# Five products instead of three ahead of batch 1's first kv, batch 3's third x block one slot earlier, and the late q groups transposed by DMA instead of TensorE

## The chip, the cores and the metric

One core of a Trainium2 chip. The metric is the device time of one execution in microseconds (us), lower is better, as the median of several runs. A profile is one execution taken by the hardware profiler; its times count from the start of its span. PE is TensorE, PEld its weight loads, DVE is VectorE, ACT is ScalarE, POOL is GpSimd, SP is the engine that issues most DMAs.

## The reference, cut to what matters

```python
# q, k, v: (8 batches, 8 heads, 576, 64); x: 4608 tokens x 512
q_s = softmax over the head dimension of q
k_s = softmax over the sequence of k
kv  = einsum('bhsd,bhse->bhde', k_s, v)
x   = einsum('bhsd,bhde->bhse', q_s, kv)      # to (tokens, 512)
h = x @ w_in                                  # 512 -> 2048
g = h + sin(alpha * h)**2 / alpha
out = g @ w_out                               # 2048 -> 512
```

## The kernel before: the parts that matter

The 4608 tokens go through the two-layer part in nine blocks of 512 ("layer blocks", `t`). The attention of a later batch is woven into the layer work of an earlier block. A "slot" is one of the sixteen 128-row pieces of h: four matmuls on PE, a sine on ACT, a square on ACT, POOL or DVE as a string of letters says, and a combine on DVE, which also frees the PSUM buffer of that h. The "kv" of a batch is its small product of k and v, an "x block" is one of four pieces of a batch's attention output x, and an "output product" is one matmul of g with w_out.

```python
def h_slot(t, ni, sq, lag, wide=None):
    hp = mm_h(t, ni, wide, 2 if t < 2 and ni < 2 else 0)      # 4 matmuls, 512 columns each
    lag.append((t, ni, hp, sine(t, ni, hp, sq)))              # ACT sine, then the square

def flush(lag, keep):
    while len(lag) > keep:
        combine(*lag.pop(0))                                  # DVE
...
        exp_to(A["qe", 1][:, 7:J], q78)          # batch 1: the last two of nine q groups come late
        take(os, 3)                              # three output products of layer block 0
        kv_mm(1, 0, ps_e, split=True)            # needs ACT's cast of the first half of v
        kv_norm(1, 0, 1)
        take(os, 3)
        kv_mm(1, 1, ps_e, split=True)
...
        norm_late(1, 7)                          # DVE: softmax of the late q groups
        load("q", q, 3)
        load("k", k, 3)
...
    take(os, 10)                                 # ten output products of layer block 1
    tp = ps_a.tile([128, 2, 2, 128], BF16, name="tp", tag="a")
    for ii in range(2):
        for j in range(2):
            nc.tensor.transpose(tp[:, ii, j], A["qe", 1][:, 7 + j, ii * 128:(ii + 1) * 128], identb)
    DVE_CP(A["qT", 1][:, :, 7:J], tp)
    take(os, 7)
...
    def attn_back(b, n, engs=(DVE_CP, DVE_CP), xs=(4, 6, 8, 10)):
        if n == 0:
            kv_mm(b, 0, ps_a)
            kv_mm(b, 1, ps_a)
            kv_norm(b)
        elif n in xs:                            # four x blocks, all in the one buffer of ps_a
            m = xs.index(n)
            attn_out(b, m // 2, m % 2, ps_a, engs[m % 2])
...
    SQ2 = "PAPPAPAPPAPAPPAP"
    for ni in range(nN):                         # layer block 2
        h_slot(2, ni, SQ2[ni], lag, lent)
        flush(lag, 2)
        attn_back(3, ni - 5, (DVE_CP, ACT_CP), (5, 7, 9, 10))
    flush(lag, 0)
```

After layer block 2, ACT loads the table for the exponential, takes the exponentials of batch 4's q and k, loads the table for the sine and starts on layer block 3. PE meanwhile starts the slots of layer block 3 in the four PSUM buffers there are; its fifth slot needs the first one combined.

The softmax here doesn't subtract the row's maximum and nothing guards it: scores larger than these inputs give would overflow.

Of the kernel before, what the change touches and what calls it, by code (L numbers as in the profile page):

```python
# [16 lines left out]
BF16 = mybir.dt.bfloat16  # L17
# [6 lines left out]
def kernel(  # L24
# [14 lines left out]
    nc = tc.nc  # L39
# [5 lines left out]
    J = 9  # L45
# [20 lines left out]
    identb = singles.tile([128, 128], BF16, name="identb")  # L66
# [10 lines left out]
    def src_view(t, b):  # L77
        return t[b].rearrange("(i e) (p j) d -> (e p) i (j d)", e=2, j=J)
# [7 lines left out]
    def load(name, t, b, halves=False, eng=nc.sync, gate=None):  # L86

        st = stage.tile([128, 4, J, D], F32, name=f"st_{name}", tag="st")
        for ii in range(2) if gate else ():
            gate(st[:, ii, 0, 0:1], zero)  # L90
        view = src_view(t, b)
        flat = st.rearrange("p i j d -> p i (j d)")
        if halves:
            for ii in range(2):
                eng.dma_start(out=flat[:, ii::2], in_=view[:, ii::2])
        else:
            eng.dma_start(out=flat, in_=view)
        staged[name, b] = st

    def load_batch(b):  # L100
        load("q", q, b)
        load("k", k, b)
        load("v", v, b)
# [6 lines left out]
    def load_wout(c):  # L110
        nc.gpsimd.dma_start(out=wout[:, 4 * c:4 * c + 4, :], in_=wout_v[:, 4 * c:4 * c + 4, :])


    A = {}

    def exp_to(dst, src, iis=range(2)):
        for ii in iis:
            nc.scalar.activation(dst[:, :, ii * 128:(ii + 1) * 128].rearrange("p j (x d) -> p x j d", x=2),  # L118
                                 src[:, ii::2], AX.Exp)
# [5 lines left out]
    def exp_half(name, b, ii, j1=J):  # L125
        if ii == 0:
            A[name + "e", b] = att2.tile([128, J, 4 * D], BF16, name=name + "e")
        exp_to(A[name + "e", b][:, 0:j1], staged[name, b][:, :, 0:j1], (ii,))

    def exp_k(b):  # L130
        A["ke", b] = att2.tile([128, J, 4 * D], BF16, name="ke")
        exp_to(A["ke", b], staged["k", b])
# [22 lines left out]
    def norm_late(b, j0):  # L155

        qe = A["qe", b][:, j0:J].rearrange("p j (i d) -> p j i d", i=4)
        qs = small.tile([128, J, 4], F32, name="qs")[:, j0:J]
        nc.vector.tensor_reduce(qs, qe, axis=AXL.X, op=ALU.add)
        nc.vector.reciprocal(qs, qs)  # L160
        nc.vector.tensor_tensor(qe, qe, qs.unsqueeze(3).to_broadcast([128, J - j0, 4, D]), op=ALU.mult)
# [119 lines left out]
    ACT_CP, DVE_CP, GP_CP = nc.scalar.copy, nc.vector.tensor_copy, nc.gpsimd.tensor_copy  # L281
# [4 lines left out]
    def load0(eng, n, t, ii, j0=0, j1=J):  # L286
        eng.dma_start(out=staged[n, 0][:, ii::2, j0:j1].rearrange("p i j d -> p i (j d)"),
                      in_=src_view(t, 0)[:, ii::2, j0 * D:j1 * D])
# [80 lines left out]
    def h_slot(t, ni, sq, lag, wide=None):  # L369
        hp = mm_h(t, ni, wide, 2 if t < 2 and ni < 2 else 0)  # L370
        lag.append((t, ni, hp, sine(t, ni, hp, sq)))

    def flush(lag, keep):
        while len(lag) > keep:
            combine(*lag.pop(0))

    def o_quad(t, accs, engs):

        R = range(4)
        by_m, by_n = [(n, m) for m in R for n in R], [(n, m) for n in R for m in R]  # L380
        orders = [by_m, by_n, by_n, by_m]
        for c in R:
            for n, m in orders[c]:
                mm_o(t, m, 4 * c + n, accs[m])
                if c == 3 and n == 3:
                    evac_o(t, m, accs[m], engs[m])
                yield

    def take(it, n=1000):
        for _ in range(n):  # L390
            if next(it, 0) == 0:
                return
# [4 lines left out]
    with ES:  # L397
        def lent():
            return ps_e.tile([128, 2, MF], F32, name="hh", tag="a")[:, 0]

        def load_q8():
            for ii in range(2):
                load0(nc.sync, "q", q, ii, 8, 9)

        def load_q1():
            staged["q", 1] = st = stage.tile([128, 4, J, D], F32, name="st_q", tag="st")
            for ii in range(2):
                DVE_CP(st[:, ii, 0, 0:1], zero)
            for ii in range(2):
                nc.sync.dma_start(out=st[:, ii::2, 0:7].rearrange("p i j d -> p i (j d)"),  # L410
                                  in_=src_view(q, 1)[:, ii::2, 0:7 * D])

        late = {4: load_q8, 6: load_q1, 8: lambda: load_wout(2),
                10: lambda: load_wout(3), 13: lambda: load("k", k, 1, halves=True, gate=DVE_CP)}
        for ni in range(nN):
            h_slot(0, ni, "DPPAPPAPPPAPPAPP"[ni], lag, lent)
            flush(lag, 1)
            if ni in late:
                late[ni]()
        flush(lag, 0)  # L420

        accs = [ps_h.tile([128, dm], F32, name="hp", tag="h") for _ in range(4)]
        os = o_quad(0, accs, [DVE_CP, ACT_CP, DVE_CP, DVE_CP])
        take(os, 46)
        exp_to(A["qe", 0][:, 8:9], staged["q", 0][:, :, 8:9])
        for ii in range(2):
            exp_half("q", 1, ii, 7)
        load("v", v, 1, halves=True)
        nc.sync.dma_start(out=q78.rearrange("p i j d -> p i (j d)"), in_=src_view(q, 1)[:, :, 7 * D:J * D])
        load_batch(2)  # L430
        norm_late(0, 8)
        norm_q(1, [GP, V], 7)
        exp_k(1)
        q_tile(1)
        for ii in range(2):
            tp = ps_e.tile([128, 16, 128], BF16, name="tp", tag="a")
            q_transpose_ii(1, ii, 0, 7, tp)
            if ii == 1:
                for i2 in range(2):
                    nc.tensor.transpose(tp[:, 8 + i2], A["qe", 0][:, 8, i2 * 128:(i2 + 1) * 128], identb)  # L440
            DVE_CP(A["qT", 1][:, ii, 0:7], tp[:, 0:7])
        DVE_CP(A["qT", 0][:, :, 8], tp[:, 8:10])
        take(os, 6)
        xp = ps_e.tile([128, 4, P], F32, name="xp", tag="a")
        for c in range(4):
            attn_chunk(0, c, 8, 9, xp[:, c])
        DVE_CP(xT[:, :, 8 * P:9 * P], xp)
        cast_v(1, [ACT_CP, DVE_CP])
        exp_to(A["qe", 1][:, 7:J], q78)
        take(os, 3)  # L450
        kv_mm(1, 0, ps_e, split=True)
        kv_norm(1, 0, 1)
        take(os, 3)
        kv_mm(1, 1, ps_e, split=True)
        kv_norm(1, 1, 2)
        take(os, 1)

        c0 = J * P
        for ii in range(2):
            xp = ps_e.tile([128, 2, 512], F32, name="xp", tag="a")[:, :, 0:7 * P]  # L460
            for e in range(2):
                attn_chunk(1, 2 * ii + e, 0, 7, xp[:, e])
            (ACT_CP, DVE_CP)[ii](xT[:, 2 * ii:2 * ii + 2, c0:c0 + 7 * P], xp)
            if ii == 0:
                nc.scalar.activation(zero, zero, AX.Sin)
            take(os, 2)
        take(os)
        norm_late(1, 7)
        load("q", q, 3)
        load("k", k, 3)  # L470

        for ki in range(2):
            for ni in range(2):
                mm_h(1, ni, lent, ki, ki + 1)
        for ni in range(nN):
            h_slot(1, ni, SQ[ni], lag, lent)
            flush(lag, 1)
        cast_v(2, [GP_CP, GP_CP])
        flush(lag, 0)

    ps_o = ctx.enter_context(tc.tile_pool(name="ps_o", bufs=2, space=PSUM, reuse_waits="tile"))
    ps_a = ctx.enter_context(tc.tile_pool(name="ps_a", bufs=1, space=PSUM, reuse_waits="tile"))
# [13 lines left out]
    exp_k(2)  # L496
    os = o_stream(1)
    take(os, 10)
    tp = ps_a.tile([128, 2, 2, 128], BF16, name="tp", tag="a")
    for ii in range(2):  # L500
        for j in range(2):
            nc.tensor.transpose(tp[:, ii, j], A["qe", 1][:, 7 + j, ii * 128:(ii + 1) * 128], identb)
    DVE_CP(A["qT", 1][:, :, 7:J], tp)
    take(os, 7)
    xp = ps_a.tile([128, 4, 2 * P], F32, name="xp", tag="a")
    for c in range(4):
# [31 lines left out]
# [5 lines that stand above are left out]
        elif n in xs:  # L543
            m = xs.index(n)
            attn_out(b, m // 2, m % 2, ps_a, engs[m % 2])
# [5 lines left out]
    for ni in range(nN):  # L551
        h_slot(2, ni, SQ2[ni], lag, lent)
        flush(lag, 2)
        attn_back(3, ni - 5, (DVE_CP, ACT_CP), (5, 7, 9, 10))
    flush(lag, 0)

    for t in range(3, nT):
        b = t + 1 if t + 1 < B else None
        os = o_stream(t - 1)
# [59 lines left out]
```

## Time and profile before

| | before |
|---|---|
| median time, first three runs | 287.75 us (287.33 to 288.11) |
| span of the profile | 285.8 us |
| PE busy | 95% |
| granted TensorE clock | 0.999 |
| PE waits after the start-up that the change aims at | 0.44 us (first kv of batch 1), 0.28 us (last x block of batch 3) |

PE is the bound in sum, so an idle tenth of a microsecond on PE is one in the total, unless a later wait of PE swallows it. Where that happens is not seen in sums: one has to lay the instructions of PE, ACT and DVE side by side. A wait in brackets behind an instruction is idle time of its engine just before it, and what ended it.

### The profile page before, as it was taken

What the parts mean: (1) busy time and instruction counts of PE and PEld (TensorE: products, weight loads), DVE (VectorE), ACT (ScalarE), POOL (GpSimd) and SP (SyncE); (2) the same over time, 40 slices, a digit from 0 to 9 for tenths busy, and PEclk for the clock granted to TensorE, in tenths of its full rate; (3) what the DMA queues carried; (4) which work ended last, traced back from release to release, by engine and by line L of the source; (5) the groups of instructions that cost most, each with busy time, mean ns of one, the idle gap of its engine ahead of it and who ended that gap; (6) DMA issues with size and microseconds to landing.
All of it is one profiled execution on the core that took longest, in us unless ns stands there. A gap on an engine that the chain in (4) does not pass through costs nothing.

```text
span 285.8 us, 4247 instructions
## 1 busy us (share of the span) xinstructions
PE 272.6 (95%) x1541; PEld 130.8 (46%) x1569; DVE 192.6 (67%) x291; ACT 226.0 (79%) x321; POOL 80.6 (28%) x75
## 2 busy tenths in 40 slices
PE   2899999999999999999999999999999999999994
PEld 1444454445454454444544454445444444444443
DVE  4857967999999658766785677667674555555321
ACT  4898748999489999899889988998877777777400
POOL 2869512773477480005300530041000000000000
PEclk9999999999999999999999999999999999999999
DMA  7999999843999984139711990016011111111242
GB/s 261 308 204 243 260 397 407 312 169 78 275 222 412 372 169 105 37 69 406 218 38 39 359 292 20 22 36 155 1 39 37 37 37 39 37 38 41 46 100 73
DMA packets 38581, 45.77 MB, mean 160 GB/s; under 512 B 16528, under 2 KB 22432, under 8 KB 38560
## 3 DMA queue, kind: packets, MB, share of 16 engines
q1 hardware_dynamic: 33376, 40.57, 46.3%
q0 software_dynamic: 4992, 4.79, 9.7%
q8 instruction: 12, 0.20, 0.3%
q10 hardware_dynamic: 192, 0.14, 0.2%
q14 instruction: 9, 0.07, 0.1%
HBM read 36.71 MB, written 9.44 MB: 161 GB/s over the span
## 4 chain that ended last, share of the span: by engine, by line
PE 74%; DVE 9%; DMA 7%; ACT 4%; issue 3%; POOL 2%; SPq 0%; ACTq 0%
PE op L268 33%; PE hp L248 33%; DMA st_v<-in_v_dram 5%; ACT s L254 3%; DVE g L264 2%; POOL s L258 2%; PE kvp L171 2%; DVE qs L150 2%; PE xp L220 2%; DMA st_q<-in_q_dram 1%; PE op L589 1%; PE hh L248 1%; DVE vb L137 1%; DVE qn L152 1%; DVE kbd L184 1%
## 5 line engine op out<-in xcount | busy, mean ns | idle before, releaser
L264 DVE SCALAR_TENSOR_TENSOR g<-s,inva_sb,hp 128x512 bf16<-128x512 f32 x130 | 96.0, 745 | 58.4 <-ACT s L256 54.2
L248 PE MATMUL hp<-xT,win 128*128 128x512 bf16 x512 | 129.0, 379 | 0.5
L268 PE MATMUL op<-wout,g 128*128 128x512 bf16 x479 | 121.9, 379 | 1.2 <-issue 0.6
L254 ACT ACTIVATE s<-hp,alpha_sb 128x512 f32<-128x512 f32 x130 | 87.8, 682 | 25.1 <-PE hp L248 22.6
L248 PEld LDWEIGHTS <-win 128*128 128x128 bf16 x576 | 56.3, 98 | 67.5 <-issue 0.8
L268 PEld LDWEIGHTS <-g 128*128 128x128 bf16 x560 | 54.1, 98 | 61.1 <-issue 0.4
L256 ACT ACTIVATE s<-s 128x512 f32<-128x512 f32 x111 | 69.9, 630 | 3.5
L152 POOL TENSOR_TENSOR qn<-qe,qs 128x1152 bf16<-128x1152 bf16 (+1 forms) x12 | 24.9, 2091 | 78.6 <-DVE qs L146 69.2
L258 POOL TENSOR_TENSOR s<-s 128x512 f32<-128x512 f32 x30 | 33.0, 1111 | 22.3 <-ACT s L254 22.0
L274 DVE COPY o<-op 128x512 f32<-128x512 f32 (+2 forms) x33 | 22.0, 668 | 9.7 <-PE op L268 5.8
L118 ACT ACTIVATE ke<-st_k 128x1152 bf16<-128x1152 f32 x16 | 17.9, 1151 | 5.0 <-DMA st_k<-in_k_dram 5.0
L118 ACT ACTIVATE qe<-st_q 128x1152 bf16<-128x1152 f32 (+3 forms) x18 | 17.7, 1025 | 2.1 <-DMA st_q<-in_q_dram 1.9
L145 DVE TENSOR_REDUCE qs<-qe 128x36 f32<-128x2304 bf16 x5 | 12.8, 2553 | 8.7 <-ACT qe L118 8.6
L268 PE MATMUL hp<-wout,g 128*128 128x512 bf16 x62 | 14.8, 379 | 0.2 <-issue 0.2
L223 DVE CAST xT<-xp 128x512 bf16<-128x512 f32 (+1 forms) x18 | 13.4, 742 | 0.0
L137 POOL CAST vb<-st_v 128x1152 bf16<-128x1152 f32 x10 | 11.3, 1163 | 6.5 <-DMA st_v<-in_v_dram 6.5
L171 PEld LDWEIGHTS <-ke 64*128 64x128 bf16 x288 | 8.4, 93 | 4.9 <-issue 1.9
L171 PE MATMUL kvp<-vb,ke 64*128 64x130 bf16 x288 | 9.9, 216 | 0.7 <-ACT vb L137 0.4
L118 ACT ACT_TABLE_LOAD x7 | 9.0, 1283 | 1.3 <-PEq L603 1.2
L248 PE MATMUL hh<-xT,win 128*128 128x512 bf16 x39 | 9.6, 379 | 0.1
L220 PE MATMUL xp<-qT,kbd 128*128 128x256 bf16 (+1 forms) x40 | 8.2, 286 | 0.4 <-DVE xT L223 0.3
L150 DVE TENSOR_REDUCE qs<-qe 128x16 f32<-128x1024 bf16 (+2 forms) x6 | 7.2, 1197 | 1.8 <-ACT qe L118 1.8
(79 smaller groups left out, 123.1 us busy)
## 6 DMA issues: line engine op xcount, KB each, us to landing
out_dram<-o SPq DMA_DIRECT2D x70, 128.0 KB, 2.3
st_q<-in_q_dram SPq DMA_DIRECT2D x6, 1152.0 KB, 6.7
st_k<-in_k_dram SPq DMA_DIRECT2D x6, 1152.0 KB, 8.9
st_v<-in_v_dram SPq DMA_DIRECT2D x6, 1152.0 KB, 10.2
st_k<-in_k_dram SPq DMA_DIRECT2D x4, 576.0 KB, 7.1
wout<-in_moe_w_out_dram POOLq DMA_DIRECT2D x4, 512.0 KB, 11.7
st_v<-in_v_dram SPq DMA_DIRECT2D x3, 576.0 KB, 9.4
win<-in_moe_w_in_dram POOLq DMA_DIRECT2D x6, 256.0 KB, 7.7
```

The costliest lines, as they stand in the source:

```text
L118: nc.scalar.activation(dst[:, :, ii * 128:(ii + 1) * 128].rearrange("p j (x d) -> p x j d", x=2), src[:, ii::2], AX.Exp)
L137: engs[ii](vv[:, 2 * ii:2 * ii + 2, :, 0:D], staged["v", b][:, ii::2])
L152: engs[ii % len(engs)].tensor_tensor(qn[:, ii, 0:j1].rearrange("p j (x d) -> p j x d", x=2), qe[:, ii], part.unsqueeze(3).to_broadcast([12 ...
L171: nc.tensor.matmul(kvp[:, e, ii * 130:(ii + 1) * 130], ke[r, j, ii * 128:(ii + 1) * 128], vt[r, j, ii * 130:(ii + 1) * 130], start=(j == 0 ...
L220: nc.tensor.matmul(xp[:, e, 0:n], kt[:, e, ii], qT[:, ii, j0:j1, e * 64:(e + 1) * 64], start=True, stop=True)
L248: nc.tensor.matmul(hp, win[:, ki, ni * 128:(ni + 1) * 128], xT[:, ki, t * MF:(t + 1) * MF], start=(ki == 0), stop=(ki == 3))
L254: nc.scalar.activation(s, hp, AX.Sin, scale=alpha_sb[:, ni:ni + 1])
L256: nc.scalar.activation(s, s, AX.Square)
L258: nc.gpsimd.tensor_tensor(s, s, s, op=ALU.mult)
L264: nc.vector.scalar_tensor_tensor(G[t][:, ni], in0=s, scalar=inva_sb[:, ni:ni + 1], in1=hp, op0=ALU.mult, op1=ALU.add)
L268: nc.tensor.matmul(acc, G[t][:, ni, j * 128:(j + 1) * 128], wout[:, ni, :], start=(ni == 0), stop=(ni == nN - 1))
L274: eng(o[:, cols], acc)
```

## The change

Its intent is to close two PE holes and to take four transposes off PE. Part 1 puts five instead of three products ahead of the kv that waits for v. Part 2 has the late q groups transposed by DMA. Part 3 moves the third x block of batch 3 one slot forward, so that the fourth need not wait for its copy.

```diff
         exp_to(A["qe", 1][:, 7:J], q78)
-        take(os, 3)
+        take(os, 5)
         kv_mm(1, 0, ps_e, split=True)
         kv_norm(1, 0, 1)
-        take(os, 3)
+        take(os, 2)
         kv_mm(1, 1, ps_e, split=True)
@@
         norm_late(1, 7)
+        for j in range(7, J):
+            nc.sync.dma_start(out=A["qT", 1][:, :, j], in_=A["qe", 1][:, j], transpose=True)
         load("q", q, 3)
@@
     take(os, 10)
-    tp = ps_a.tile([128, 2, 2, 128], BF16, name="tp", tag="a")
-    for ii in range(2):
-        for j in range(2):
-            nc.tensor.transpose(tp[:, ii, j], A["qe", 1][:, 7 + j, ii * 128:(ii + 1) * 128], identb)
-    DVE_CP(A["qT", 1][:, :, 7:J], tp)
     take(os, 7)
@@
-        attn_back(3, ni - 5, (DVE_CP, ACT_CP), (5, 7, 9, 10))
+        attn_back(3, ni - 5, (DVE_CP, ACT_CP), (5, 7, 8, 10))
```

## The prediction

> **What bounds the kernel now.** I read the page from the top. The engine shares first:
>
> ```profile
> PE 272.6 (95%) x1541; PEld 130.8 (46%) x1569; DVE 192.6 (67%) x291; ACT 226.0 (79%) x321; POOL 80.6 (28%) x75
> ...
> PE 74%; DVE 9%; DMA 7%; ACT 4%; issue 3%; POOL 2%; SPq 0%; ACTq 0%
> ```
>
> TensorE (PE) is busy for 95% of 285.8 us and makes 74% of the chain that ended last. The granted clock is 0.999, so throttling plays no part. The change adds no matmul and takes away four small transposes, so the question is only how much PE idle time it removes or makes. The waits of PE alone answer how much there is:
>
> ```profile
> PE warm L308 <- DMA alpha_rows<-in_moe_alpha_dram: 3.0, 1, 3.0
> PE warm L329 <- ACT qe L118: 2.3, 1, 2.3
> PE xp L228 <- DVE kbd L184: 0.9, 1, 0.9
> PE op L268 <- issue: 0.6, 4, 0.2
> PE kvp L171 <- ACT vb L137: 0.4, 1, 0.4
> PE xp L220 <- DVE xT L223: 0.3, 1, 0.3
> ```
>
> The first three are start-up, which the change leaves alone. It aims at two of the rest: the wait of batch 1's first kv product for the cast of v, and the wait of batch 3's last x block for the copy of the block before it. Together they are 0.7 us of 287.75, or 0.25%. Whatever happens, this is a change of tenths of a microsecond. The timeline of PE between 40 and 46 us shows the first one:
>
> ```profile
> 40.84 0.81 PE L268 MATMUL hp<-wout,g 128*128 128x512 bf16 x3
> 42.09 0.69 PE L171 MATMUL kvp<-vb,ke 64*128 64x130 bf16 x18 [0.44 <-ACT vb L137]
> ```
>
> The three output products start at 40.84 us, one every 0.216 us (ten of the 512-column matmuls in a row show that spacing), so a fourth could start at 41.49 us. The kv starts at 42.09 us, when ACT's cast (40.87 us + 1.17) is done. The true hole is 0.60 us; the 0.44 is less because an entry is drawn longer than the spacing.
>
> **What the Trainium skill says.** "TensorE: Matmul & The Clock Gate", section "Step-by-step: what each phase is for", gives a gap of about 216 ns for 512 columns; the trace agrees (0.216). "Perfetto Trace Analysis", section "Tensor Engine Instruction (MATMUL, LD_WEIGHTS)", says that the profiler computes the end of a matmul rather than observing it. That agrees with matmuls drawn 0.38 us long at 0.216 us spacing, and is why I work with starts. "VectorE: DVE Perf Modes", section "The three transpose paths", puts a 128x128 bf16 transpose at 390 ns on TensorE and 1309 ns by DMA, and advises TensorE if PSUM will do. Here four TensorE transposes are drawn 0.219 us each but hold PE only from 62.11 to 62.34 us, so 0.23 us for all. The DMA transposes here are of 9 or 18 blocks and take 2.9 us to land on an idle queue, 5.3 us in the median. "DMA: Bandwidth & Descriptors", section "Issuing engines are not separate DMA queues", says that all DMAs end up on the same 16 engines and interleave; the bulk loads here fill those engines from 38 to 52 us (DMA share 1.02 to 1.08 in 2 us windows), just ahead of the new transposes.
>
> **Part 1, five products before the first kv.** Two more products, 2 x 0.216 = 0.43 us, fit in the 0.60 us hole. One comes out from between the two kv and one from the end of the stage, so the next layer's products start 0.43 us earlier. I checked that nothing there becomes the gate. The second v cast on DVE is done at 43.07 us and the second kv would move from 43.46 to 43.24. The x copies on ACT and DVE depend on attention products that come 0.22 us earlier; the DVE one would end about 46.5 us against a need at 46.56, so it is tight. Gain: **0.43 us**.
>
> **Part 2, the late q groups by DMA.** PE loses four transposes (0.23 us) and DVE one copy (0.42 us, at 63.15). But look at the products just after:
>
> ```profile
> 62.49 0.75 DVE L264 SCALAR_TENSOR_TENSOR g<-s,inva_sb,hp 128x512 bf16<-128x512 f32 x1 [0.44 <-POOL s L258]
> 63.15 0.42 DVE L503 COPY qT<-tp 128x512 bf16<-128x512 bf16 x1
> 63.29 0.23 PEld L268 LDWEIGHTS <-g 128*128 128x128 bf16 x2 [0.21 <-DVE g L264]
> ```
>
> The weight load of the stream's sixteenth product already waits for DVE's last combine, which ends at 63.24 us; its matmul starts at 63.42 us, right behind. Without the transposes PE would be there 0.23 us sooner and wait 0.2 us for the combine, which hangs on ACT's sine and POOL's square. DVE's saved copy lies ahead of an output copy that waits for PE anyway. Gain: **about 0**. The transposes are issued on SP at about 52.2 us, where the q and k loads of batch 3 stood. Those start one to three microseconds later (issue of a 9-block transpose is 1.3 to 1.4 us); they landed at 58.0 and 60.9 us and are read from 66.9 us. Needed at 63.2 us, the transposes should land by 58. Hidden.
>
> **Part 3, batch 3's third x block one slot earlier.** All four blocks use one PSUM buffer, so a block waits until the one before is copied out.
>
> ```profile
> 89.40 0.43 PE L220 MATMUL xp<-qT,kbd 128*128 128x320 bf16 x2
> 90.27 0.68 ACT L223 CAST xT<-xp 128x640 bf16<-128x640 f32 x1
> 90.84 1.44 ACT L254 ACTIVATE s<-hp,alpha_sb 128x512 f32<-128x512 f32 x2
> 91.39 0.38 PE L220 MATMUL xp<-qT,kbd 128*128 128x256 bf16 x2
> 92.92 0.43 PE L220 MATMUL xp<-qT,kbd 128*128 128x320 bf16 x2 [0.28 <-DVE xT L223]
> ```
>
> In these times of before: the third block moves from behind slot 14 (91.39) to behind slot 13, at 89.67 + 0.86 = 90.53 us. ACT frees the buffer at 90.27 + 0.68 = 90.95. So the third block waits until 91.01, a hole of 0.48. The fourth stays behind slot 15 and no longer waits (its true hole was 92.92 - 92.48 = 0.44). On PE the holes cancel: fourth block at 91.01 + 0.22 + 2 x 0.86 = 92.95 against 92.92.
>
> But slot 14's products now start at 91.01 + 0.22 = 91.23 instead of 90.53, 0.70 us later, and ACT's sine of that slot needs them. ACT has no slack here:
>
> ```profile
> 92.31 0.63 ACT L256 ACTIVATE s<-s 128x512 f32<-128x512 f32 x1
> 92.85 0.67 ACT L254 ACTIVATE s<-hp,alpha_sb 128x512 f32<-128x512 f32 x1
> 93.42 0.68 ACT L223 CAST xT<-xp 128x640 bf16<-128x640 f32 x1
> 94.12 1.28 ACT L118 ACT_TABLE_LOAD   x1
> 95.41 2.22 ACT L118 ACTIVATE qe<-st_q 128x1152 bf16<-128x1152 f32 x2
> 97.53 2.20 ACT L118 ACTIVATE ke<-st_k 128x1152 bf16<-128x1152 f32 x2
> 99.75 1.28 ACT L254 ACT_TABLE_LOAD   x1
> 101.05 0.69 ACT L254 ACTIVATE s<-hp,alpha_sb 128x512 f32<-128x512 f32 x1
> ```
>
> It runs without a hole from there through two table loads and four exponentials to layer block 3's first sine and square. Then DVE combines and frees the first of four PSUM buffers at 102.43 + 0.75 = 103.18 us, and PE's fifth slot starts at 103.23 us though its own work would have let it start at 102.68 + 2 x 0.216 = 103.11. The profile books no PE wait for it because of the drawn ends, but PE follows ACT there. So ACT's 0.70 us goes straight through to PE: **a loss of about 0.70 us**. Afterwards ACT needs 1.24 us a slot against PE's 1.43 and catches up; nothing is given back, as PE is full to the end.
>
> **Sum.** 287.75 - 0.43 - 0 + 0.70 = 288.0 us.
>
> **Rivals.** (a) The hole simply closes: if the start at 103.23 is chance and ACT has more slack there than I think, only part 1 counts, 287.3 us; for it speaks that the chain of waits runs through PE in that stretch and that the profile names no wait. Against it: 103.18 and 103.23 agree too well, and the instruction stream has that matmul waiting for DVE. (b) The full intent: 0.43 + 0.23 + 0.28 = 0.94 us, 286.8; against it speak the weight load waiting for DVE at 63.29 and ACT's copy at 90.27. (c) The DMA transposes land late behind the backlog, or push the loads of q and k behind ACT's exponentials at 66.9. There are more than five microseconds to spare, but if it failed, PE would stand for a microsecond or more: above 289.
>
> **Range and chances.** The mechanism of part 3 I hold at some 60%, rival (a) at 25 to 30%, the others for little. Weighted, 0.6 x 288.0 + 0.3 x 287.3 with the rest about even is near 287.8; I say 287.9, leaning to the mechanism. The three runs of before spread over 0.8 us, so 287.1 to 288.6 holds both main cases with noise. Two per cent is 5.8 us, six times the most that any part can win and more than a late load would cost: within 2% at 97%.
>
> **What would show it.** Part 1: PE's wait for the v cast gone, batch 1's first layer products 0.43 us earlier (46.14 to about 45.7). Part 2: a new PE wait for DVE's combine of about 0.2 us near 63 us. Part 3: a wait of the third x block for ACT's copy instead of the fourth's for DVE's; a hole of 0.7 to 0.8 us in ACT ahead of its sine of slot 14; and PE's fifth slot of layer block 3 starting 0.2 to 0.3 us later than 103.23. I am wrong if that fifth slot starts earlier than 103.0, if PE shows a wait for a DMA near 63 us, or if ACT waits for q or k of batch 3.

## The result and the profile after

The changed kernel took 288.46 us (287.72 to 288.78, six runs), the kernel before 287.76 us (six runs). The ratio is 1.0022, with a 95% interval from 1.0005 to 1.0038: slightly slower. (A ratio is the mean time of one kernel's runs over that of the other's of the same rounds, so it is not quite the ratio of the medians.) The result lies within the predicted range, 0.56 us above the predicted time.

The page after, engine shares and chain of waits: PE is as busy as before.

```profile
PE 272.6 (95%) x1537; PEld 130.5 (46%) x1565; DVE 193.2 (67%) x290; ACT 225.9 (79%) x321; POOL 80.1 (28%) x75
```

The waits of PE after: the wait for batch 1's v cast (L137) is gone, a start-up wait (L316) has grown from 0.2 to 0.9 us, and two are new. PE waits 0.3 us for ACT's copy of an x block where it waited for DVE's, and 0.6 us for DVE's combine at a slot.

```profile
PE kvp L171 <- ACT vb L316: 0.9, 1, 0.9
...
PE hp L248 <- DVE g L264: 0.6, 1, 0.6
PE xp L220 <- ACT xT L223: 0.3, 1, 0.3
```

ACT's timeline at the end of layer block 2, after: where it had run without a hole, it now stands 0.74 us ahead of the sine of slot 14 (92.60), waiting for PE.

```profile
90.59 0.68 ACT L223 CAST xT<-xp 128x640 bf16<-128x640 f32 x1
91.16 0.70 ACT L254 ACTIVATE s<-hp,alpha_sb 128x512 f32<-128x512 f32 x1
92.60 0.69 ACT L254 ACTIVATE s<-hp,alpha_sb 128x512 f32<-128x512 f32 x1 [0.74 <-PE hp L248]
93.32 0.63 ACT L256 ACTIVATE s<-s 128x512 f32<-128x512 f32 x1
93.86 0.67 ACT L254 ACTIVATE s<-hp,alpha_sb 128x512 f32<-128x512 f32 x1
```

PE's timeline after: the third x block waits for ACT's copy (90.59 + 0.68 = 91.27), and 12.9 us later the fifth slot of layer block 3 waits for DVE.

```profile
91.32 0.38 PE L220 MATMUL xp<-qT,kbd 128*128 128x256 bf16 x2 [0.31 <-ACT xT L223]
...
104.24 1.02 PE L248 MATMUL hp<-xT,win 128*128 128x512 bf16 x4 [0.61 <-DVE g L264]
```

The chain that ended last, between 90 and 104.5 us, ties the two together (start, length, what). Before, this stretch of the chain ran through PE from 92.92 us on; now it goes from ACT's copy over the x block and slot 14 to ACT, through both table loads, and comes back to PE only at 104.24 us.

```profile
90.59 0.69 ACT xT L223
91.28 0.04 issue
91.32 0.38 PE xp L220 x2
91.70 0.88 PE hp L248 x4
92.58 0.02 issue
92.60 0.69 ACT s L254
...
103.44 0.76 DVE g L264
104.20 0.04 issue
```

**Marks instead of totals.** Times from the start of the span cannot be compared directly, because the start-up differs from run to run: batch 0's first kv began at 9.80 us before and at 10.72 us after, on the same instructions. So I divide each profile by six marks on PE: batch 0's first kv, the four small matmuls of batch 0's last x block (40.73 us before), the first product of layer block 1 (46.14), batch 3's kv (81.70), the fifth slot of layer block 3 (103.23) and the start of the last group of products (278.27). The four stretches between the last five of them hold one disputed thing each: A the hole ahead of kv (part 1), B the transposes (part 2), C the x blocks (part 3), D the rest.

| profile | first kv | A | B | C | D |
|---|---|---|---|---|---|
| before | 9.80 | 5.41 | 35.56 | 21.53 | 175.04 |
| after | 10.72 | 4.91 | 35.47 | 22.21 | 175.04 |

From before to after the changes sum to -0.50 - 0.09 + 0.68 + 0 = +0.09 us. The second mark itself comes 0.92 us later, all of it start-up. That gives the 1.01 us by which the last group of products starts later (279.28 against 278.27). What the change did is thus mixed with what the run did, and the -0.50 of stretch A is itself suspect: the timeline of kv after shows that v was ready early.

```profile
40.43 1.17 ACT L137 CAST vb<-st_v 128x1152 bf16<-128x1152 f32 x1 [0.20 <-DMA st_v<-in_v_dram]
...
41.77 1.24 PE L268 MATMUL hp<-wout,g 128*128 128x512 bf16 x5
42.94 0.68 PE L171 MATMUL kvp<-vb,ke 64*128 64x130 bf16 x18
```

The cast ended at 41.60 us, before even the first of the five products. With three of them kv would not have waited in this run either.

### The profile page after: what moved, and what is told of

Same layout as the page of the kernel before. It is cut to its first block, busy times and chain, and to the rows that moved or that the text cites. A ratio compares the mean times of both kernels' runs of the same rounds, so it can differ in the third digit from the quotient of the medians.

```text
span 286.6 us, 4241 instructions
## 1 busy us (share of the span) xinstructions
PE 272.6 (95%) x1537; PEld 130.5 (46%) x1565; DVE 193.2 (67%) x290; ACT 225.9 (79%) x321; POOL 80.1 (28%) x75
## 4 chain that ended last, share of the span: by engine, by line
PE 80%; DVE 7%; DMA 4%; ACT 4%; issue 2%; SPq 1%; ACTq 0%
PE hp L248 35%; PE op L268 31%; PE hp L268 5%; PE hh L248 3%; PE kvp L171 2%; DMA st_v<-in_v_dram 2%; DMA st_q<-in_q_dram 2%; DVE g L264 2%; PE xp L220 1%; DVE qs L150 1%; ACT s L254 1%; PE op L586 1%; DVE vb L137 1%; ACT qe L118 1%; ACT ke L118 1%
## 5 line engine op out<-in xcount | busy, mean ns | idle before, releaser
L137 POOL CAST vb<-st_v 128x1152 bf16<-128x1152 f32 x10 | 11.3, 1162 | 6.9 <-DMA st_v<-in_v_dram 6.9
L118 ACT ACT_TABLE_LOAD x7 | 9.0, 1283 | 1.3 <-PEq L600 1.2
```

The source lines that it names most:

```text
L118: nc.scalar.activation(dst[:, :, ii * 128:(ii + 1) * 128].rearrange("p j (x d) -> p x j d", x=2), src[:, ii::2], AX.Exp)
L137: engs[ii](vv[:, 2 * ii:2 * ii + 2, :, 0:D], staged["v", b][:, ii::2])
```

## The experiments

**My theory:** part 3 costs about 0.7 us, because ACT is the limit from slot 14 of layer block 2 to the fifth slot of layer block 3. Parts 1 and 2 each save a little, part 1 only in runs where v comes late. **Rivals:** the start-up is later in the changed kernel for a reason of its own, or the DMA transposes cost the time and part 3 is neutral on PE. All twelve runs gave correct results; all timed comparisons use five rounds, and no run counted as slow (the single one of `e9_before_again` has no state).

### One part at a time

`e1_part1` keeps only the first hunk of the diff above, `e2_part2` only the two about the transposes, `e3_part3` only the last line, `e4_parts12` all but the last line.

> Part 1 alone (five products ahead of batch 1's first kv). Theory of the prediction: the hole ahead of kv closes and the whole run is up to 0.43 us faster than before (287.3). Second thought after the trace of the changed kernel: v there was cast 1.34 us before kv began, so the hole is not always there; then the gain is between 0 and 0.43 us by the run, on average about 0.2. Rival 'start-up': the start of the program differs by 0.9 us between two profiles for reasons of its own; in this profile kv follows the products without a wait, whatever the start-up was.

> Part 2 alone (late q groups of batch 1 transposed by DMA). Theory: hidden; 0 to 0.2 us faster, because PE loses 0.23 us of transposes but then stands 0.05 us behind DVE's last combine near 63 us. Rival 'the DMA transposes cost the time': this kernel alone is 0.6 us slower than before.

> Part 3 alone (third x block of batch 3 one slot earlier). Theory: 0.7 us slower than before; in the profile a hole of 0.7 us or more in ACT ahead of the sine of slot 14, a PE wait for ACT's copy of the second block, and a wait of about 0.6 us of PE for DVE's combine at the fifth slot of layer block 3. Rival 'the holes on PE cancel': 0 us.

> The change without part 3. Theory: 0.2 to 0.6 us faster than before, hence 0.7 to 0.9 us faster than the changed kernel; no PE wait for DVE's combine at the fifth slot of layer block 3. Rival 'start-up or DMA transposes': as slow as the changed kernel (0.6 us slower than before).

| kernel | median, us | ratio to before (95%) | first kv | A | B | C | D |
|---|---|---|---|---|---|---|---|
| before, same rounds | 287.85 | | | | | | |
| part 1 alone | 287.84 | 0.9991 (0.9978 to 1.0004) | 10.52 | 4.91 | 35.62 | 21.52 | 175.04 |
| part 2 alone | 287.60 | 0.9990 (0.9978 to 1.0002) | 10.72 | 4.91 | 35.45 | 21.53 | 175.04 |
| part 3 alone | 288.46 | 1.0020 (1.0008 to 1.0032) | 9.85 | 5.85 | 35.57 | 22.21 | 175.05 |
| parts 1 and 2 | 287.07 | 0.9975 (0.9962 to 0.9987) | 10.14 | 5.01 | 35.48 | 21.52 | 175.05 |

Stretch C is 22.21 us in both kernels with part 3 and 21.52 to 21.53 in the others: **part 3 costs 0.68 us**, and its own timing (1.0020, 0.58 us) is the only one of the single parts clear of noise. Stretch B is 0.08 to 0.11 us shorter than before in the kernels with part 2, and 0.06 us longer with part 1 alone. Stretch A settles part 1. It is 4.91 us also in the kernel with part 2 alone, which has only three products ahead of kv; there v was early. It is 5.85 us with part 3 alone, where v was later than in the profile of before. So 4.91 us is the floor, and part 1 can win only what the run's v leaves above it. With parts 1 and 2 it is 5.01 us, five products and still 0.10 us of hole: in that run part 1 won its whole 0.43 us. The two rivals fall: the late start-up (10.52, 10.72) is met in kernels that are not slower, and part 2 alone is not slower.

### Is it ACT that sets the time there?

`e5_after_sq14` is the changed kernel, `e6_parts12_sq14` the one without part 3, each with one letter changed, so that POOL instead of ACT squares slot 14. `e7_parts12_even` and `e8_parts12_even_sq14` space the x blocks evenly, without and with that letter.

```diff
-    SQ2 = "PAPPAPAPPAPAPPAP"
+    SQ2 = "PAPPAPAPPAPAPPPP"          # e5, e6, e8
-        attn_back(3, ni - 5, (DVE_CP, ACT_CP), (5, 7, 9, 10))
+        attn_back(3, ni - 5, (DVE_CP, ACT_CP), (4, 6, 8, 10))    # e7, e8
```

> The changed kernel with the square of slot 14 of layer block 2 moved from ACT to POOL. If ACT's uninterrupted row from that slot to the first sine of layer block 3 sets the time, the 0.54 us that the square holds ACT come off the end: about 0.5 us faster than the changed kernel, so level with before, and the wait for DVE's combine at the fifth slot falls from 0.61 to under 0.1 us. Rival 'ACT has slack, the loss is the PE hole ahead of the third block': no change, 0.6 us slower than before, as that hole stays.

> The same move of the square in the kernel without part 3 (third block at its old place). There PE follows ACT by only 0.11 us, so the theory gives 0.1 us of gain against the kernel without part 3, five times less than the same edit gives in the changed kernel. Rival 'a square less on ACT is worth its time anywhere': 0.5 us of gain.

> Parts 1 and 2 with the four x blocks evenly behind every second slot (4, 6, 8, 10), so that no block should wait for a copy for more than 0.2 us. Theory: PE reaches the end of layer block 2 about 0.45 us sooner, but the third block still stands ahead of slot 14, which starts 0.2 us later for ACT; PE then waits for ACT at the fifth slot and the whole is 0.2 us slower than the kernel without part 3. Rival 'PE holes are what counts': 0.45 us faster than it.

> Even places and the square of slot 14 on POOL together. Theory: ACT reaches layer block 3 0.35 us sooner (0.54 less 0.19) and PE is there in time: 0.35 us faster than the kernel without part 3, 1.0 us faster than before. If the two edits do not add up like this (0.1 us or less gained), ACT's row is not what is in the way.

| kernel | median, us | ratio to before (95%) | first kv | A | B | C | D |
|---|---|---|---|---|---|---|---|
| before, same rounds | 287.84 | | | | | | |
| after, square on POOL | 288.19 | 1.0009 (0.9995 to 1.0022) | 10.71 | 4.91 | 35.46 | 21.84 | 175.04 |
| parts 1 and 2, square on POOL | 287.62 | 0.9991 (0.9978 to 1.0005) | 10.91 | 4.91 | 35.47 | 21.50 | 175.05 |
| parts 1 and 2, even places | 288.01 | 1.0011 (0.9993 to 1.0029) | 10.62 | 4.91 | 35.47 | 21.67 | 175.05 |
| the same, square on POOL | 287.29 | 0.9979 (0.9965 to 0.9994) | 11.41 | 4.91 | 35.47 | 21.29 | 175.05 |

Taking one square off ACT shortens stretch C by 0.37 us in the changed kernel (22.21 to 21.84) and by 0.02 us in the one without part 3 (21.52 to 21.50). With even places it takes off 0.38 us (21.67 to 21.29). The same edit is worth its time where ACT came late, and next to nothing where it did not: that fits the theory, and the rival of `e5_after_sq14` falls, because the PE hole ahead of the third block stayed. The size was off: 0.37 and not 0.54 us, because ACT then catches up with PE, as the last sine of the block and the fifth slot of the next show in the timelines of `e5_after_sq14`.

```profile
93.45 0.69 ACT L254 ACTIVATE s<-hp,alpha_sb 128x512 f32<-128x512 f32 x1 [0.18 <-PE hp L248]
...
103.85 1.02 PE L248 MATMUL hp<-xT,win 128*128 128x512 bf16 x4 [0.24 <-DVE g L264]
```

In `e6_parts12_sq14` the 0.02 us (0.1 expected) has another reason than the expected one. ACT spent the saved time idle, 0.40 us ahead of slot 15's sine, and then had to copy the fourth block, which still waits for DVE's copy of the third:

```profile
93.21 0.69 ACT L254 ACTIVATE s<-hp,alpha_sb 128x512 f32<-128x512 f32 x1 [0.40 <-PE hp L248]
93.92 0.69 ACT L223 CAST xT<-xp 128x640 bf16<-128x640 f32 x1
```

Counted from batch 3's kv, its table load comes only 0.02 us sooner than in `e4_parts12` (12.39 against 12.41 us), and the fifth slot still follows DVE's combine (end at 102.94 + 0.75 = 103.69, start at 103.74). So this run does not measure how far PE could have come sooner.

The even places by themselves made stretch C 0.15 us longer than in `e4_parts12` (0.2 expected), although the holes ahead of the third and fourth block were gone: the third block still stands ahead of slot 14 and delays ACT (0.19 us idle ahead of that sine). With the square on POOL as well, stretch C is 0.23 us shorter than in `e4_parts12` and the time 0.55 us under before; 0.35 and 1.0 us were expected, and ACT again stood 0.18 us ahead of the last sine. The even places rest on a hole that I had overlooked: before, the second block at 89.40 us could have started at 88.24 + 0.86 = 89.10, and waited 0.3 us for DVE's copy of the first, which the list of waits does not name.

### What the start-up does, and a faster version

`e9_before_again` is the kernel before, unchanged, for one look; `e10_after_again` and `e11_parts12_again` repeat two kernels in the same rounds. `e12_best` adds to `e8_parts12_even_sq14` a swap of the copying engines, so that the fourth block is copied by DVE.

```diff
-        attn_back(3, ni - 5, (DVE_CP, ACT_CP), (4, 6, 8, 10))
+        attn_back(3, ni - 5, (ACT_CP, DVE_CP), (4, 6, 8, 10))
```

> The kernel before, unchanged, for a second profile. Across nine profiles batch 0's first kv started between 9.80 and 11.41 us and the cast of batch 1's v ended between 41.6 and 43.0 us. If that is chance of the run, this profile differs from the first in both by some tenths, and only the stretches between the marks agree: from batch 3's kv to the fifth slot of layer block 3 again 21.5 us, from there to the last product again 175.0. If it belonged to the program, all marks would fall as in the first profile.

> The changed kernel again, beside the next two on the same chip. Theory: 22.2 us from batch 3's kv to the fifth slot whatever the start-up is, and 0.1 to 0.6 us slower than before. Rival 'its start-up is always late': first kv again at 10.7 us.

> The change without part 3 again, because its first timing (0.7 us faster than before) is more than the 0.2 to 0.6 us of the theory. Theory: 0.3 to 0.7 us faster than before and about 0.7 us faster than the changed kernel of the same rounds.

> Parts 1 and 2, even places (4, 6, 8, 10), square of slot 14 on POOL, and the copies' engines swapped, so that the last x block is copied by DVE and ACT goes to its table load 0.57 us sooner. There PE waited 0.24 us (0.40 counted from starts) for DVE's combine at the fifth slot: theory 0.3 to 0.4 us off the 21.29 us from batch 3's kv to the fifth slot, so about 20.9, and 1.0 us or more faster than before. If the last block's copy on DVE comes too late for the first product of layer block 3, PE waits there for DVE instead and nothing is gained.

| kernel | median, us | ratio to before (95%) | first kv | A | B | C | D |
|---|---|---|---|---|---|---|---|
| before, same rounds | 288.07 | | | | | | |
| before again (one run) | 288.32 | | 10.59 | 4.91 | 35.56 | 21.53 | 175.04 |
| after again | 288.32 | 1.0005 (0.9988 to 1.0022) | 10.35 | 4.91 | 35.47 | 22.22 | 175.05 |
| parts 1 and 2 again | 287.86 | 1.0003 (0.9975 to 1.0031) | 10.44 | 4.91 | 35.47 | 21.54 | 175.04 |
| best | 287.01 | 0.9955 (0.9938 to 0.9972) | 10.69 | 4.91 | 35.47 | 20.89 | 175.05 |

The second profile of the kernel before starts its first kv at 10.59 us, not at 9.80, and has no hole ahead of batch 1's kv: its three products are followed by kv without a wait.

```profile
42.12 0.81 PE L268 MATMUL hp<-wout,g 128*128 128x512 bf16 x3
42.87 0.68 PE L171 MATMUL kvp<-vb,ke 64*128 64x130 bf16 x18
```

Start-up and hole belong to the run, and stretches B, C and D to the program: they repeat within 0.02 us. Timing a few tenths is another matter. The changed kernel came out at 1.0005 here and at 1.0022 before, and the one without part 3 at 1.0003 (with one run at 290.25 us) and at 0.9975 before; only its median, 0.46 us under the changed kernel's, agrees in sign with the stretches, which give 0.68. That it would be 0.3 to 0.7 us faster than before did not come true in these rounds (0.21 us by medians). I trust the stretches for the size and take from the timings that the signs fit.

`e12_best` has 20.89 us in stretch C, as expected, and no PE wait left there in the list of waits; by the starts 0.21 us still stand ahead of the second block (88.87 against 86.93 + 8 x 0.216 = 88.66). It has the lowest ratio of all, 0.45% faster than before, and its median is 1.31 us under the changed kernel's of the same rounds. Stretches B and C account for 0.73 us of its 1.06 us under before (by medians); the other 0.33 us may come from stretch A, where part 1 can win up to 0.43 us by the run; no profile of these timings shows it.

## Why the prediction was right

- **What bounds.** Right: PE's busy time did not move (272.6 us in both), and all differences are tenths of a microsecond.
- **Part 3, loss of 0.70 us.** Right in mechanism and size. Measured: 0.68 us in stretch C, an ACT hole of 0.74 us ahead of slot 14's sine, the third block waiting for ACT's copy, and PE standing 0.61 us at the fifth slot. The fourth block starts 0.03 us later relative to the first, as worked out (92.95 against 92.92). Moving one square (`e5_after_sq14` against `after`) shows that ACT's row carries the delay to PE: 0.37 us came back while the hole on PE stayed. The reading that PE followed ACT at 103.23 us already before, which no wait in the profile names, stands too. Before:

```profile
102.43 0.75 DVE L264 SCALAR_TENSOR_TENSOR g<-s,inva_sb,hp 128x512 bf16<-128x512 f32 x1 [1.80 <-ACT s L256]
...
102.68 0.59 PE L268 MATMUL op<-wout,g 128*128 128x512 bf16 x2
103.23 1.02 PE L248 MATMUL hp<-xT,win 128*128 128x512 bf16 x4
```

In `e12_best`, where the combine is done earlier (102.03 + 0.75 = 102.78 us), the fifth slot starts right behind its two products, at 102.58 + 2 x 0.216 = 103.01 us; before, it started 0.12 us later than that sum.

- **Part 1, gain of 0.43 us.** The term that was mis-sized. I took the hole of one profile for a property of the program. Its far end is the landing of v, its near end PE's progress, and both vary. Of the four profiles without part 1 two have a hole (A at 5.41 and 5.85 us, so 0.50 and 0.94 over the floor) and two have none. Part 1 can win at most 0.43 us in the first two and nothing in the others: about 0.2 us on average, an estimate from these four. In the profile after it won nothing. The check of what becomes the gate was off as well: the copy of x on DVE, called tight, is the gate now. Measured ends and needs meet (46.33 + 1.09 = 47.42 us against 46.56 + 4 x 0.216 = 47.42), and the sixteen matmuls from 46.56 us take 3.50 us (to 50.06) instead of 3.45 (46.14 to 49.59). So part 1 gives back 0.05 us in stretch B.
- **Part 2, about 0.** 0.11 us gained by itself (`e2_part2`), and 0.14 to 0.15 us beside part 1 (35.62 in `e1_part1` against 35.47 and 35.48). The step that DVE's combine gates the sixteenth product was nearly right. In the profile after, seventeen products from 60.42 us would end at 60.42 + 17 x 0.216 = 64.09, and the attention block starts at 64.17: 0.08 us was lost of the 0.23 us saved, less than I said, and no wait of 0.2 us is named. Relative to the combine, PE had 0.1 us more room than I read. The DMA side was right: the loads of batch 3's q and k went out at 54.96 and 55.58 us, landed 5.8 and 8.0 us later and were read from 67.32 us on. No run shows PE waiting for a transpose.
- **Sum.** With the measured terms it is -0.2 - 0.1 + 0.68 = +0.4 us over before; the two timings say +0.6 and +0.1. The prediction's own sum was +0.27. It named 287.9 us instead of 288.0 because it mixed in rival (a), which the fifth slot refutes: no run with part 3 starts it without a wait. Rivals (b) and (c) did not happen. The range of 287.1 to 288.6 also holds the time of before (287.76), so a time within it shows little by itself; what bears the prediction out is stretch C.
- **The check that could mislead.** "The fifth slot 0.2 to 0.3 us later than 103.23" came out as 1.01 us later, of which 0.92 us is start-up. A mark has to be measured from a mark near it.

Left open: why the start-up varies. In fourteen profiles batch 0's first kv begins between 9.80 and 11.41 us. It waits for the first loads and their casts, but no experiment changed those.

## What to carry to other kernels

When two engines take turns at being the limit, an instruction moved forward on the first delays all that it jumps over; ask whose input that is before counting the hole that it closes. A wait that the profile shows once may belong to the run: measure the same stretch in several profiles, from a nearby mark, before taking its size into a sum. And starts show what drawn ends hide: PE's dependence on ACT at the fifth slot, and the hole ahead of the second block, are in no list of waits.

## What the Trainium skill lacked or had wrong

- "VectorE: DVE Perf Modes", section "The three transpose paths", gives one time per 128x128 transpose. Here the DMA path hardly took longer for nine blocks than for two: a DMA transpose of two blocks held SP's queue for 1.23 to 1.28 us and landed in 2.4 us, one of nine blocks 1.29 to 1.39 us and 2.9 us; those of eighteen blocks took 1.87 to 3.99 us and 4.0 to 7.5 us. On TensorE four in a row held PE for 0.23 us in all, so the section's 390 ns for one does not tell what PE gives up.
- "ScalarE: Activation LUTs", section "What ACT_TABLE_LOAD costs", adds a drain of some 1380 ns to a load of 1283 ns. The load agrees (1.28 us); the drain is not seen: the copy ahead of it ends at 95.11 us, the load runs from 95.13 us, and the exponential starts at 96.42 us.
- No page that I read says that a list of waits made from drawn ends shows a PE hole too small by the time by which a 512-column matmul is drawn longer than its spacing (0.38 against 0.216 us), here 0.44 us for 0.60 between starts, and can pass over one: the 0.30 us ahead of the second block (89.10 to 89.40) are not in it.
- No page that I read says how much the start of a program varies: batch 0's first kv, which waits for the first loads and their casts, varies by 1.6 us over fourteen profiles of near-identical start-ups, more than any part of this change.
